# Moving half of a weight load from GpSimd's DMA queue to SyncE's, with the rounding on ScalarE

## The chip, the core and the metric

The kernel runs on one core of a Trainium2 chip. A core has five engines that run their own instruction streams in order and meet at semaphores: TensorE (PE, matrix products), VectorE (DVE), ScalarE (ACT), GpSimd (POOL) and SyncE (SP), which here only issues DMAs. Sixteen DMA engines move data between the chip's memory (HBM) and the core's on-chip memory (SBUF). The metric is the device time of one execution in microseconds; the profile also gives the span from the first to the last instruction.

## What is computed

The input is q, k and v with batch 8, 8 heads, 576 positions and head size 64, all float32. Two attentions are added: one on means over groups of 4 positions, repeated 4 times, and one at full length in a band of 3 positions to each side. The sum, as 4608 tokens of 512 numbers, goes through two products with a SiLU between them.

```python
q_d = q.reshape(B, H, Sd, 4, D).mean(axis=3)           # k_d, v_d the same
out_up = np.repeat(softmax(scale * q_d @ k_d.T) @ v_d, 4, axis=2)
mask = np.abs(pos[:, None] - pos[None, :]) < 4
out_local = softmax(np.where(mask, scale * q @ k.T, -1e9)) @ v
x = (out_up + out_local) as (4608, 512)
h = x @ w_in                                            # w_in (512, 2048)
out = (h / (1 + exp(-h))) @ w_out                       # w_out (2048, 512)
```

## The kernel before

The attention runs over 32 pairs of heads. For each pair p SyncE loads q and k (`lq`, `lk`, 288 KB each) and v in four overlapping windows (`lv`, `lv.1` to `lv.3`, 80 KB each, tile `vs`). GpSimd casts q and k to bf16 (`c`, line 544, tile `qkb`) and v (`cw`, line 554, tile `vb`), and adds pairs of q for the means (`mq`, lines 597 and 599). TensorE transposes (`T`), and ScalarE takes the result out of PSUM (`eq`, `ek`). TensorE makes the scores (`S`), ScalarE the exponentials (`x`, `xd`), VectorE masks them (`k`, line 628), TensorE makes the softmax sums (`Z`) and the products with v (`PV`; `VP` with `ev` makes the means of v). VectorE inverts the sums (`r`) and, for the first ten pairs, splits the inverse into three bf16 parts (`rx`, `rm`, `rl`, lines 711 to 714, with `rh` on ScalarE); TensorE broadcasts them (`RB`), ScalarE copies the broadcast out (`eb`, line 735, tile `Rb`). VectorE multiplies (`m`, line 745, tile `xo`), and GpSimd adds the two attentions into the token tile `xT` (`a`, line 769).

The feed-forward part takes blocks j of 512 tokens: 16 products `g1_j_f` (4 matmuls each, over the quarters kc of the 512 inputs) give 128 hidden rows f each. Each needs the tanh `t` on ScalarE (line 783) and the product `s` on VectorE (line 785), which fills `gT[j % 2]`. Then `g2` multiplies with w_out. Only two PSUM tiles, HP, take turns for `g1`.

The weights come as eight DMAs issued by GpSimd (`load_w`, line 520): `w0` to `w3` bring 512 columns of w_in each, 1 MB, into `w_in_sb`, whose type float32r is a float32 rounded for TensorE, and `w4` to `w7` bring w_out as bf16. `g1_j_f` waits for the chunk f // 4.

The order on every engine is made ahead of the run. `Plan` keeps units of work with an engine, an estimated cost, a priority and an earliest time (`ready`); `order` walks through simulated time, picks for each engine the best of its next units, and then each engine's stream is emitted in that order. A list in `FIRST` for an engine fixes its first units by name; in this kernel `FIRST` is empty. The name of a unit that comes several times gets a suffix, so `lv5.3` is the fourth `lv5`. The order that results around 20 to 50 us, for what follows:

- SyncE: per pair `lq lk lv lv.1 lv.2 lv.3`, pairs in turn
- GpSimd: `... c4 w0 cw3 mq3 c5 a0 cw4 mq4 w1 c6 a1 cw5 mq5 a2 w2 c7 cw6 mq6 a3 c8 cw7 w3 a4 ...`
- ScalarE: `... eq5 ek5 eb2 rh3 ev3 x4 xd4 eq6 ek6 eb3 rh4 ev4 x5 xd5 eq7 ek7 eb4 rh5 ev5 t0_0 t0_1 x6 ...`
- TensorE: `... S4 T6 PV3 RB3 Z4 VP4 S5 T7 Z5 RB4 VP5 PV4 g1_0_0 g1_0_1 S6 ...`
- VectorE: `... r3 mk5 m2 rx3 rm3 rl3 k4 r4 mk6 rx4 m3 rm4 k5 rl4 r5 mk7 rx5 m4 rm5 rl5 s0_0 s0_1 ...`

Of the kernel before, what the change touches and what calls it, by code (L numbers as in the profile page):

```python
# [276 lines left out]
def bass_hourglass_attn__then__act_silu_kernel(  # L277
# [9 lines left out]
    with kctx:  # L287
# [16 lines left out]
        xT = sb("xT", [128, 4, XR], F32)
        gT = sb("gT", [128, 16, 512], BF16, 2)
# [45 lines left out]
        rH = [R("h0", True), R("h1", True)]  # L351

        def one(eng, name, cost, fn, r=(), w=(), dma=None, prio=None, dcost=0.0):
            u = L.unit(eng, name, cost, prio, dcost)
            L.op(u, fn, r, w, dma)
            return u

        def mm(u, out_, lhsT, rhs, r, w, start=True, stop=True):
            L.op(u, lambda t: t.matmul(out_, lhsT, rhs, start=start, stop=stop, skip_group_check=True), r, w)  # L359
# [103 lines left out]
        def dma(eng, name, out_, in_, w, sem, dcost, r=(), prio=None, cost=0.42):  # L463
            return one(eng, name, cost, lambda s: s.dma_start(out_, in_), r, w, sem, prio, dcost)  # L464
# [42 lines left out]
        def load_vq(p):  # L507
# [67 lines left out]
        def after_T(p):  # L575
# [163 lines left out]
        def xblk(kc, t0, t1):  # L739
            return [R(f"x{kc}_{t % (XR // 64)}") for t in range(t0 // 64, t1 // 64)]  # L740
# [33 lines left out]
        def g1(j, f):  # L774
            n = ng1[0]
            ng1[0] += 1
            hb, tb = n % 2, n % 2
            t0 = (512 * j) % XR
            u = L.unit("PE", f"g1_{j}_{f}", 0.934)
            for kc in range(4):  # L780
                mm(u, hps[hb], w_in_sb[:, kc, 128 * f:128 * f + 128], xT[:, kc, t0:t0 + 512].bitcast(F32R),
                   [R(f"w_in{f // 4}")] + xblk(kc, 512 * j, 512 * j + 512), [rH[hb]], start=(kc == 0), stop=(kc == 3))
            one("ACT", f"t{j}_{f}", 0.62, lambda e: e.activation(th[tb][:, :], hps[hb], AF.Tanh, scale=0.5),  # L783
                r=[rH[hb]], w=[R(f"th{tb}")], prio=-1)
# [71 lines left out]
        def feed():  # L856

            for p in range(NPAIR):
                for name, fn, need in (
                    ("lqk", load_qk, ("c", NQK)), ("c", cast, ("T", NB - 1)),  # L860
                    ("lv", load_v, ("cw", NVS)), ("cw", castw, ("PV", NV)),
                    ("lvq", load_vq, ("cv", NVQ)), ("cv", castv, ("PV", NV)),
                ):
                    src = {"c": "lqk", "cw": "lv", "cv": "lvq"}.get(name)
                    if p < NVP and name in ("lvq", "cv"):
                        made.add((name, p))
                    if (name, p) in made or (src and (src, p) not in made):
# [105 lines left out]
```

The softmax here doesn't subtract the row's maximum and nothing guards it: scores larger than these inputs give would overflow.

## Time and profile before

| | before |
|---|---|
| device time, median of 3 (lowest, highest) | 358.56 us (356.95, 358.87) |
| span of the profiled execution | 356.2 us |
| busy: PE, DVE, ACT, POOL | 327.2, 228.1, 181.8, 156.8 us |
| chain that ended last: PE, DVE, DMA, SyncE's queue, ACT | 79, 7, 4, 4, 3% |
| w_in chunks: issues, size, median to landing | 4, 1024 KB, 10.6 us |
| the same, w_out chunks | 4, 512 KB, 11.2 us |
| vs loads: issues, size, median to landing | 126, 80 KB, 4.2 us |
| moved by DMA | 60.28 MB |

In the profile's lines L12 means line 12 of the kernel, "out<-in" names the tiles, and "[3.55 <-X]" says that the engine stood idle for 3.55 us before this instruction, until X released it. A timeline row has start, length, engine, line, operation, tiles, shapes and count. DMA issues on SyncE are told as "SPq"; "landing" is the time from the start of the issue to the completion.

### The profile page before, as it was taken

What the parts mean: (1) busy time and instruction counts of PE and PEld (TensorE: products, weight loads), DVE (VectorE), ACT (ScalarE), POOL (GpSimd) and SP (SyncE); (2) the same over time, 40 slices, a digit from 0 to 9 for tenths busy, and PEclk for the clock granted to TensorE, in tenths of its full rate; (3) what the DMA queues carried; (4) which work ended last, traced back from release to release, by engine and by line L of the source; (5) the groups of instructions that cost most, each with busy time, mean ns of one, the idle gap of its engine ahead of it and who ended that gap; (6) DMA issues with size and microseconds to landing.
All of it is one profiled execution on the core that took longest, in us unless ns stands there. A gap on an engine that the chain in (4) does not pass through costs nothing.

```text
span 356.2 us, 11025 instructions
## 1 busy us (share of the span) xinstructions
PE 327.2 (92%) x4742; PEld 212.7 (60%) x4742; DVE 228.1 (64%) x392; ACT 181.8 (51%) x326; POOL 156.8 (44%) x203
## 2 busy tenths in 40 slices
PE   1574599899999999999999999999999999999996
PEld 0453477666666666666666665666665666666642
DVE  7589889876667777777776766677754434343400
ACT  2766478766554555555555554555543343434321
POOL 7977874272374675664667367555111100000000
PEclk9998689999999999999999999999999999999999
DMA  8999999946878877778887987873222000110012
GB/s 230 248 264 243 302 297 219 220 131 179 235 193 237 223 225 223 221 201 226 233 227 193 229 240 206 194 182 107 65 111 77 31 29 29 51 39 29 31 59 88
DMA packets 73506, 60.28 MB, mean 169 GB/s; under 512 B 47986, under 2 KB 55794, under 8 KB 73458
## 3 DMA queue, kind: packets, MB, share of 16 engines
q1 hardware_dynamic: 63818, 44.27, 47.5%
q10 hardware_dynamic: 5416, 9.02, 8.7%
q0 software_dynamic: 4224, 6.29, 7.5%
q8 instruction: 37, 0.61, 0.7%
q14 instruction: 11, 0.09, 0.1%
HBM read 51.76 MB, written 9.91 MB: 173 GB/s over the span
## 4 chain that ended last, share of the span: by engine, by line
PE 79%; DVE 7%; DMA 4%; SPq 4%; ACT 3%; issue 2%; POOL 1%; POOLq 0%; ACTq 0%; DVEq 0%
PE HP L359 35%; PE o L359 25%; PE pe_ L359 8%; PE CD L359 5%; SPq L464 4%; PE AB L359 3%; DMA vq<-in_v_dram 3%; PE o L572 1%; DVE rrest L711 1%; DVE rp L714 1%; DMA vs<-in_v_dram 1%; DVE Pt L628 1%; DVE xo L745 1%; DVE zr L707 1%; DVE gT L785 1%
## 5 line engine op out<-in xcount | busy, mean ns | idle before, releaser
L785 DVE SCALAR_TENSOR_TENSOR gT<-th,HP 128x512 bf16<-128x512 f32 x144 | 96.6, 684 | 101.2 <-ACT th L783 100.8
L359 PE MATMUL HP<-xT,w_in_sb 128*128 128x512 f32 x576 | 160.0, 416 | 1.6 <-DVE gT L785 0.7
L783 ACT ACTIVATE th<-HP 128x512 f32<-128x512 f32 x144 | 86.2, 599 | 75.3 <-PE HP L359 73.4
L359 PEld LDWEIGHTS HP<-xT,w_in_sb 128*128 128x128 f32 x576 | 106.0, 189 | 28.9 <-DVE gT L785 1.3
L359 PE MATMUL o<-w_out_bf,gT 128*128 128x512 bf16 x464 | 107.0, 380 | 0.0
L359 PEld LDWEIGHTS o<-w_out_bf,gT 128*128 128x128 bf16 x464 | 42.6, 98 | 54.3 <-issue 8.6
L769 POOL TENSOR_TENSOR xT<-xo 128x576 fp32r<-128x576 f32 (+3 forms) x48 | 42.9, 907 | 44.5 <-DVE xo L745 44.5
L800 ACT ACTIVATE osb<-o 128x512 f32<-128x512 f32 x29 | 17.4, 599 | 60.4 <-PE o L359 60.3
L559 POOL TENSOR_TENSOR vt<-vq 128x512 f32<-128x512 f32 x18 | 23.0, 1278 | 56.0 <-DMA vq<-in_v_dram 55.9
L544 POOL CAST qkb<-qk 128x1152 bf16<-128x1152 f32 x30 | 36.8, 1226 | 6.9 <-PE pe_ L572 4.7
L745 DVE TENSOR_TENSOR xo<-CD,Rb 128x720 f32<-128x720 f32 x30 | 27.0, 899 | 1.0 <-ACT Rb L735 0.6
L554 POOL CAST vb<-vs 128x640 bf16<-128x640 f32 x30 | 22.1, 736 | 11.3 <-PE CD L359 5.6
L572 PE MATMUL o<-idn,qkb 64*64 64x64 bf16 x576 | 17.4, 202 | 9.9 <-DVE qkb L539 6.3
L359 PE MATMUL pe_<-w_out_bf,gT 128*128 128x512 bf16 x112 | 26.4, 380 | 0.0
L586 DVE TENSOR_REDUCE kd<-kT 128x144 bf16<-128x576 bf16 x32 | 23.3, 731 | 0.9 <-ACT kT L582 0.8
L582 ACT ACTIVATE kT<-pe_ 128x576 bf16<-128x576 bf16 x32 | 21.0, 655 | 1.9
L628 DVE TENSOR_TENSOR Pt<-Pt,mask_bf 128x576 bf16<-128x576 bf16 x32 | 20.7, 647 | 0.8 <-ACT Pt L624 0.8
L624 ACT ACTIVATE Pt<-AB 128x576 bf16<-128x576 f32 x32 | 20.7, 646 | 0.6 <-PE AB L359 0.4
L572 PEld LDWEIGHTS o<-idn,qkb 64*64 64x64 bf16 x576 | 13.9, 117 | 9.7 <-DVE qkb L539 6.3
L572 PE MATMUL pe_<-idn,qkb 64*64 64x64 bf16 x576 | 16.3, 202 | 2.0 <-DVE qkb L541 1.0
L359 PEld LDWEIGHTS pe_<-w_out_bf,gT 128*128 128x128 bf16 x112 | 10.0, 98 | 13.6 <-issue 3.2
L590 DVE TENSOR_REDUCE qd<-qT 128x144 bf16<-128x576 bf16 x24 | 17.8, 742 | 0.0
(79 smaller groups left out, 311.9 us busy)
## 6 DMA issues: line engine op xcount, KB each, us to landing
vs<-in_v_dram SPq DMA_DIRECT2D x126, 80.0 KB, 4.2
qk<-in_q_dram SPq DMA_DIRECT2D x32, 288.0 KB, 3.6
out_dram<-osb SPq DMA_DIRECT2D x36, 256.0 KB, 3.3
qk<-in_k_dram SPq DMA_DIRECT2D x30, 288.0 KB, 4.8
Rb<-scr ACTq DMA_DIRECT2D x44, 180.0 KB, 4.2
vq<-in_v_dram SPq DMA_DIRECT2D x18, 256.0 KB, 5.2
w_in_sb<-in_moe_w_in_dram POOLq DMA_DIRECT2D x4, 1024.0 KB, 10.6
w_out_bf<-in_moe_w_out_dram POOLq DMA_DIRECT2D x4, 512.0 KB, 11.2
```

What stands on the lines that cost most here:

```text
L359: L.op(u, lambda t: t.matmul(out_, lhsT, rhs, start=start, stop=stop, skip_group_check=True), r, w)
L544: one("POOL", f"c{p}", 1.15, lambda g: g.tensor_copy(qkb[j][:, :, :], qk[i][:, :, :]), r=[R(f"qk{i}0"), R(f"qk{i}1")], w=[R(f"qkb{j}0"), R ...
L554: one("POOL", f"cw{p}", 0.72, lambda g: g.tensor_copy(vb[m][:, :, :], vs[i][:, :, :]), r=rr, w=[R(f"vb{m}")])
L559: one("POOL", f"va{p}", 1.3, lambda g: g.tensor_tensor(vt[:, :, :], vq[i][:, :, 0:128], vq[i][:, :, 128:256], ALU.add), r=rr, w=[R("vt")])
L572: L.op(u, lambda e, o=o, w=w, j=j: e.transpose(o, w, idn[half(j), :]), [R("id"), R(f"qkb{n}{x}")], [rE if x else rF])
L582: one("ACT", f"ek{p}", 0.68, lambda e: e.activation(kT[j][:, 3:579].rearrange("p (g r) -> p g r", r=9), pe_[:, 0:288].bitcast(BF16).rearra ...
L586: one("DVE", f"mk{p}", 0.74, lambda e: e.tensor_reduce(kd[j][:, 0:SD], kT[j][:, 3:579].rearrange("p (g r) -> p g r", r=4), AX.X, ALU.add), ...
L628: one("DVE", f"k{p}", 0.46, lambda e: e.tensor_tensor(Pt[m][:, :, :], Pt[m][:, :, :], mask_bf[:, :].unsqueeze(1).to_broadcast([128, 2, 288 ...
L745: one("DVE", f"m{p}", 0.92, prio=-450000 if L.boost else None, r=rCD + [R(f"Rb{u}0"), R(f"Rb{u}1")], w=[R(f"xo{x}")], fn=lambda e: e.tenso ...
L769: one("POOL", f"a{p}", 0.15 + n * 0.0019, lambda g, dst=dst, in0=in0, in1=in1: g.tensor_tensor(dst, in0, in1, ALU.add), r=[R(f"xo{x}")], w ...
L783: one("ACT", f"t{j}_{f}", 0.62, lambda e: e.activation(th[tb][:, :], hps[hb], AF.Tanh, scale=0.5), r=[rH[hb]], w=[R(f"th{tb}")], prio=-1)
L785: one("DVE", f"s{j}_{f}", 0.71, lambda e: e.scalar_tensor_tensor(gT[j % 2][:, f, :], th[tb][:, :], 1.0, hps[hb], ALU.add, ALU.mult), r=[rH ...
```

## The change

The first two of the four chunks of w_in no longer come through GpSimd. Each comes as four plain float32 loads of 128 rows by 512 columns (256 KB) on SyncE's queue (`wi0`, `wi0.1` to `wi1.3`), placed among the loads of pairs 5 to 7. They land in the storage of `gT[0]`, which holds nothing until the first `s`, and ScalarE copies each with a rounding to float32r into its place in `w_in_sb` (`wr0` to `wr1.3`). `g1` now waits for each quarter kc by itself. GpSimd issues `w2` to `w7` only. The purpose is to take work from GpSimd and large transfers from among the attention's loads. `FIRST` is filled with a list per engine that covers the head of the kernel.

```diff
+NWH = 2
+WK = 1
+WSTEP = 2.0
+WT0 = 20.0
+WPRIO = 2000
 FIRST = {
+    "PE": """
...
+        VP4 S5 T7 Z5 RB4 g1_0_0 VP5 PV4 g1_0_1 S6 T8 g1_0_2 g1_0_3 RB5 Z6 g1_0_4 S7 g1_0_5 PV5 VP6 g1_0_6
...
+    "ACT": """
...
+        eb1 rh2 ev2 x3 xd3 eq5 ek5 wr0 eb2 rh3 wr0.1 ev3 wr0.2 x4 xd4 wr0.3 eq6 ek6 wr1 eb3 rh4 wr1.1 ev4
+        wr1.2 x5 xd5 wr1.3 eq7 ek7 eb4 rh5 ev5 t0_0 t0_1 x6 xd6 eq8 t0_2 t0_3 eb5 ek8 rh6 t0_4 x7 xd7 t0_5
...
+    "POOL": """
...
+        cw2 c4 cw3 mq3 c5 a0 cw4 mq4 c6 a1 cw5 mq5 a2 w2 c7 cw6 mq6 a3 c8 cw7 w3 a4 mq7 c9 cw8 w4 c10 w5 a5
...
+    "SP": """
...
+        lq4 lk4 lv3 lv3.1 lv3.2 lv3.3 lq5 lk5 lv4 lv4.1 lv4.2 lv4.3 lq6 lk6 wi0 lv5 lv5.1 wi0.1 lv5.2 lv5.3
+        wi0.2 lq7 lk7 wi0.3 lv6 lv6.1 wi1 lv6.2 lv6.3 wi1.1 lq8 lk8 wi1.2 lv7 lv7.1 wi1.3 lv7.2 lv7.3 lq9
...
 }
...
+        def load_w_in(c, a, ready):
+            i = 8 * c + 2 * a
+            d = w_in_sb[:, a:a + WK, 512 * c:512 * c + 512]
+            st = gT[0][:, i:i + 2 * WK, :].rearrange("p a b -> p (a b)").bitcast(F32).rearrange("p (a b) -> p a b", b=512)
+            sr = [R(f"g0_{f}") for f in range(i, i + 2 * WK)]
+            src = moe_w_in[128 * a:128 * a + 128 * WK, 512 * c:512 * c + 512].rearrange("(kc p) f -> p kc f", p=128)
+            dma("SP", f"wi{c}", st, src, sr, f"wi{c}_{a}", 0.82 * WK, prio=-1000).ready = ready
+            one("ACT", f"wr{c}", 0.12 + 0.43 * WK, lambda e: e.activation(d, st, AF.Copy), r=sr, w=[R(f"w_in{c}_{a}")],
+                prio=WPRIO)
...
         def load_w(c):
             if c < 4:
...
-                           [R(f"w_in{c}")], f"w_in{c}", 3.1, cost=0.9)
+                           [R(f"w_in{c}_{a}") for a in range(0, 4, WK)], f"w_in{c}", 3.1, cost=0.9)
...
-                   [R(f"w_in{f // 4}")] + xblk(kc, 512 * j, 512 * j + 512), [rH[hb]], start=(kc == 0), stop=(kc == 3))
+                   [R(f"w_in{f // 4}_{kc // WK * WK}")] + xblk(kc, 512 * j, 512 * j + 512), [rH[hb]], start=(kc == 0), stop=(kc == 3))
...
-        for c in range(8):
+        for i in range(4 * NWH // WK):
+            load_w_in(i * WK // 4, i * WK % 4, WT0 + WSTEP * i * WK)
+        for c in range(NWH, 8):
             load_w(c).ready = float((18, 25, 32, 39, 50, 56, 62, 68)[c])
```

More of the change, by code (lines that the diff above doesn't have):

```diff
@@ L164 @@
 FIRST = {
+    "PE": """
+        T0 T1 S0 T2 S1 Z0 VP0 T3 Z1 RB0 PV0 VP1 S2 T4 PV1 RB1 Z2 VP2 S3 T5 PV2 Z3 RB2 VP3 S4 T6 PV3 RB3 Z4
+        VP4 S5 T7 Z5 RB4 g1_0_0 VP5 PV4 g1_0_1 S6 T8 g1_0_2 g1_0_3 RB5 Z6 g1_0_4 S7 g1_0_5 PV5 VP6 g1_0_6
+        RB6 T9 Z7 g1_0_7 g1_0_8 S8 PV6 VP7 g1_0_9 g1_0_10 RB7 T10 Z8 g1_0_11 g1_0_12 S9 PV7 VP8 g1_0_13
+        g1_0_14 RB8 g1_0_15 g1_1_0 g1_1_1 V10 g1_1_2 g1_1_3 VP9 g2_0_0_0 g2_0_0_1 g2_0_0_2 RB9 g2_0_0_3
+        g1_1_4 g1_1_5 V11 g1_1_6 g1_1_7 VP10 g2_0_1_0 g2_0_1_1""",
@@ new lines @@
+    "ACT": """
+        lkx lk0 ckx eq0 ek0 cw0 eq1 ek1 cw1 x0 xd0 eq2 ek2 x1 xd1 ev0 rh0 eq3 ek3 eb0 rh1 ev1 x2 xd2 eq4 ek4
+        eb1 rh2 ev2 x3 xd3 eq5 ek5 wr0 eb2 rh3 wr0.1 ev3 wr0.2 x4 xd4 wr0.3 eq6 ek6 wr1 eb3 rh4 wr1.1 ev4
+        wr1.2 x5 xd5 wr1.3 eq7 ek7 eb4 rh5 ev5 t0_0 t0_1 x6 xd6 eq8 t0_2 t0_3 eb5 ek8 rh6 t0_4 x7 xd7 t0_5
+        ev6 t0_6 eb6 eq9 ek9 rh7 t0_7 t0_8 x8 xd8 ev7 t0_9 t0_10 eb7 eq10 ek10 rh8 t0_11 t0_12 x9 xd9 ev8
+        t0_13 t0_14 eb8 t0_15 t1_0 t1_1 eq11 ek11 rh9 t1_2 t1_3 x10 xd10 ev9 eb9 o0_0 t1_4 t1_5 ek12 x11 z10
+        t1_6 t1_7 xd11""",
@@ new lines @@
+    "DVE": """
+        const const.1 const.2 const.3 const.4 const.5 const.6 const.7 const.8 const.9 const.11 const.10
+        const.12 const.14 const.13 const.15 const.16 const.17 const.18 const.19 const.20 const.21 const.22
+        const.23 zero const.24 const.25 const.37 const.38 const.39 const.40 const.41 const.67 const.70
+        const.68 const.71 cq0 const.26 const.27 cq1 ck0 ck1 const.62 const.63 const.64 const.65 mk0 mk1 k0
+        mk2 r0 k1 rx0 rm0 rl0 r1 mk3 m0 rx1 rm1 rl1 k2 r2 mk4 rx2 m1 rm2 k3 rl2 r3 mk5 m2 rx3 rm3 rl3 k4 r4
+        mk6 rx4 m3 rm4 k5 rl4 r5 mk7 rx5 m4 rm5 rl5 s0_0 s0_1 k6 mq8 s0_2 r6 s0_3 mk8 rx6 s0_4 rm6 k7 rl6 m5
+        s0_5 s0_6 r7 mq9 mk9 rx7 s0_7 rm7 s0_8 rl7 k8 m6 s0_9 s0_10 r8 mq10 mk10 rx8 s0_11 rm8 s0_12 rl8 k9
+        m7 s0_13 s0_14 s0_15 s1_0 s1_1 r9 m8 mk11 rx9 s1_2 rm9 s1_3 rl9 mq11 k10 s1_4 s1_5 r10 eq12 mk12
+        mq12 s1_6""",
@@ new lines @@
+    "POOL": """
+        const.28 const.31 const.29 const.32 const.30 const.33 const.34 const.35 const.36 const.66 const.69
+        const.42 const.43 const.44 const.45 const.46 const.47 const.48 const.49 const.50 const.51 const.52
+        const.53 const.54 const.55 const.56 const.57 const.58 const.59 const.60 const.61 mq0 c2 mq1 c3 mq2
+        cw2 c4 cw3 mq3 c5 a0 cw4 mq4 c6 a1 cw5 mq5 a2 w2 c7 cw6 mq6 a3 c8 cw7 w3 a4 mq7 c9 cw8 w4 c10 w5 a5
+        w6 cw9 w7 a6 a7 c11 cw10 c12 cw11 cw12 c13 a8 a8.1 a8.2 c14 cw13""",
@@ new lines @@
+    "SP": """
+        lq0 lq1 lk1 lv0.1 lv0.2 lv0.3 lq2 lv0e lv0 lk2 lv1 lv1.1 lv1.2 lv1.3 lq3 lk3 lv2 lv2.1 lv2.2 lv2.3
+        lq4 lk4 lv3 lv3.1 lv3.2 lv3.3 lq5 lk5 lv4 lv4.1 lv4.2 lv4.3 lq6 lk6 wi0 lv5 lv5.1 wi0.1 lv5.2 lv5.3
+        wi0.2 lq7 lk7 wi0.3 lv6 lv6.1 wi1 lv6.2 lv6.3 wi1.1 lq8 lk8 wi1.2 lv7 lv7.1 wi1.3 lv7.2 lv7.3 lq9
+        lk9 lv8 lv8.1 lv8.2 lv8.3 lq10 lk10 lv9 lv9.1 lv9.2 lv9.3 lq11 lk11 lv10 lv10.1 lv10.2 lv10.3 lv11
+        lv11.1 lv11.2 lv11.3 lq12 lk12 lq13 lk13 lv12 lv12.1 lv12.2 lv12.3 lq14 lk14 lv13 lv13.1 lv13.2
+        lv13.3 out0_0 lq15 lk15 lv14 lv14.1 lv14.2""",
```

## The prediction

> **What bounds the kernel now.** I read the page first, its strip of 40 slices (8.9 us each):
>
> ```profile
> PE   1574599899999999999999999999999999999996
> ...
> PEclk9998689999999999999999999999999999999999
> DMA  8999999946878877778887987873222000110012
> ```
>
> TensorE is full from the ninth slice on, the DMA engines only up to there. The table by stretches sharpens it (after span and length: busy time of PE, PEld, DVE, ACT and POOL, then the granted clock, DMA share, GB/s):
>
> ```profile
> 20.00:30.00 10.00, 7.38 (x288) 6.07 (x285) 8.45 (x16) 7.41 (x16) 5.97 (x9) 1.00 1.13 270
> 30.00:40.00 10.00, 5.06 (x187) 4.09 (x187) 8.78 (x10) 4.91 (x12) 9.18 (x12) 0.66 1.24 276
> 40.00:50.00 10.00, 7.09 (x136) 5.69 (x137) 8.79 (x13) 4.95 (x11) 7.90 (x10) 0.83 1.23 284
> ...
> 76.00:200.00 124.00, 124.00 (x1981) 81.31 (x1981) 90.70 (x145) 68.02 (x122) 70.19 (x80) 1.00 0.76 209
> ```
>
> From 76 us on TensorE has no hole for 124 us, and only 0.67 us of them in 200 to 300. So a microsecond won or lost before about 50 us reaches the end at full value, and nothing later matters. In 30 to 50 us TensorE lacks 4.94 + 2.91 = 7.9 us, at clocks of 0.66 and 0.83. I followed the timelines of the engines there. GpSimd:
>
> ```profile
> 23.60 1.20 POOL L769 TENSOR_TENSOR xT<-xo 128x576 fp32r<-128x576 f32 x1
> 28.35 0.77 POOL L554 CAST vb<-vs 128x640 bf16<-128x640 f32 x1 [3.55 <-DMA vs<-in_v_dram]
> ...
> 30.19 0.78 POOL L464 DMA_DIRECT2D w_in_sb<-in_moe_w_in_dram  x1
> 30.97 1.16 POOL L544 CAST qkb<-qk 128x1152 bf16<-128x1152 f32 x1
> ...
> 33.91 0.65 POOL L597 TENSOR_TENSOR vt<-qT 128x288 f32<-128x288 bf16 x1
> 34.64 0.42 POOL L599 TENSOR_TENSOR qd<-vt 128x144 bf16<-128x144 f32 x1
> ```
>
> GpSimd stands 3.55 us for the values of pair 4, then runs without a gap. VectorE beside it:
>
> ```profile
> 31.00 3.66 DVE L711 SCALAR_TENSOR_TENSOR rrest<-rp,sgn,zr 128x72 f32<-128x72 bf16 x1
> ...
> 35.16 1.16 DVE L714 SCALAR_TENSOR_TENSOR rp<-rp,sgn,rrest 128x72 bf16<-128x72 bf16 x1
> ```
>
> The same two operations take 0.28 us elsewhere (26.77 and 28.26 us). The chain of waits passes through both ("31.08 3.59", then 1.17 us); they hold the broadcast RB3, which starts at 36.37. ScalarE sits idle behind it:
>
> ```profile
> 37.19 0.77 ACT L735 ACTIVATE Rb<-AB 128x720 f32<-128x720 f32 x1 [3.29 <-PE AB L359]
> ...
> 44.10 0.77 ACT L735 ACTIVATE Rb<-AB 128x720 f32<-128x720 f32 x1 [2.72 <-PE AB L359]
> ...
> 47.32 0.60 ACT L783 ACTIVATE th<-HP 128x512 f32<-128x512 f32 x1 [2.02 <-PE HP L359]
> ```
>
> These are eb3, eb4 and t0_0; the first product s0_0 follows at 47.95. Last, the landing of vs loads issued in 13 to 18 us and in 18 to 22 us:
>
> ```profile
> DMA to landing us min/median/max: 2.6/3.4/3.8
> ...
> DMA to landing us min/median/max: 7.1/7.4/7.7
> ```
>
> Between them GpSimd issued w0 (19.40 us, landed 7.9 us later): a megabyte in front of pair 4.
>
> **What the skill says.** "DMA: Bandwidth & Descriptors", section "SWDGE vs HWDGE vs iDMA": a float32r destination always casts, and only GpSimd's DMAs cast; hence the detour over a plain load and ScalarE. Same page, "Queues, rings and completion order": the write that completes a DMA lands after every earlier write of that DMA engine, across queues. The trace agrees: lv4.1, issued while w0 was, landed at 27.10, and w0 at 27.27. "SBUF — State Buffer", "Who interferes with whom": a VectorE instruction with two SBUF inputs blocks against a GpSimd instruction that reads SBUF; PE and ACT wait for nobody. The trace agrees: rrest reads rp and zr from SBUF, and its 3.66 us end in GpSimd's one small gap (34.56 to 34.64). "ScalarE: Activation LUTs", "What ACT_TABLE_LOAD costs": an ACTIVATE takes 186 + 0.833 N ns and overlaps the next by 93, so 613 ns for N = 512, 520 in a row. The trace has 599 for a 128x512 copy out of PSUM; none from SBUF.
>
> **The change, part by part.** *GpSimd loses w0 and w1*: 0.91 + 0.78 us of issuing. More comes from the landing. Pair 4's last load goes out at 21.06 to 21.74; with 3.4 to 4.1 us, as before w0, it lands at about 25.2 and cw4 runs then, not at 28.35: 3.1 us. With w1's 0.78, c6 can start near 27.2, not 30.97 (its k load, issued 22.85, lands near 26.8 without w0): 3.8 us. T6, which waits 1.6 us for c6, no longer does. GpSimd has a hole again where it waits for pair 5 (landing near 30), so rx3 should be blocked for at most one or two casts, some 0.3 to 1.3 us in place of 3.66. Together RB3 could start near 33.2 instead of 36.37: 3.2 us gained there.
>
> *SyncE gains eight issues*. A row of the same shape, an output store of 128x512 f32, takes 0.47 us, with gaps 0.51: 8 x 0.51 = 4.1 us. Between lk6 (end 23.29) and wi1.3 stand 14 old issues, which took 11.2 us before (23.34 to 34.48), 2.3 us of it pauses. So wi1.3 goes out between 36.2 and 38.5; I take 37. The bytes are the same 2 MB; they no longer come as two lumps.
>
> *ScalarE gains eight casts*: 8 x 0.52 = 4.2 us, in a stretch (28 to 48 us) where it idles 0.44 + 1.00 + 3.29 + 0.43 + 0.22 + 2.72 + 2.02 = 10.1 us, so the work itself would hide. The waits need not. ScalarE is in order: behind wr0.1 stands ev3 (for T6), behind wr1 eb3 (for S5 and m3), behind wr1.2 x5 (for k5, Z5), behind wr1.3 eq7, ek7 and then eb4, on which m4 and S6 wait. The early ones are free or cost one cast: wi0 to wi0.2 land by 31, at the time they are read. The late ones set the pace. A load lands 3.4 to 4.1 us after issue where nothing is in front, 8 to 11 us where a GpSimd megabyte is (8.0 in 31 to 36 us, 11.2 in 36 to 41). GpSimd now issues w2 some 3 us sooner, near 33, ahead of wi1.2 and wi1.3. So wi1.3 lands between 36.2 + 4 = 40.2 and 38 + 8 = 46; I take 37 + 6 = 43.
>
> *Then* wr1.3 ends at 43.6, eq7 and ek7 (0.53 each) at 44.7, eb4 at 45.5, against 44.87 before: the 3.2 us are spent, 0.6 more too. *g1_0_0 goes ahead of VP5 and PV4*: before, t0_0 waited 2.02 us while PE ran VP5, PV4 and g1 in turn. Now g1_0_0 is done by 45 and t0_0 can follow rh5 and ev5 at 46.1. s0_0 has m4 (0.91, from 45.6), rm5 and rl5 (0.29, or 1.26 if blocked) ahead on VectorE: 47.0 unblocked against 47.95, near 1 us sooner. I add 0.3 for a GpSimd with less to issue. *The pinned order* repeats the order of before save for these insertions, read off the lists; it costs nothing by itself. *Separate waits for each quarter of w_in, staging in the first g buffer*: nothing, since s0_0 writes it long after wr0 has read it.
>
> Sum: 1.3 us sooner, 358.56 - 1.3 = 357.3.
>
> **The rivals.** A: *the landings keep up*. If w2 doesn't get ahead of them (40.2 for wi1.3), eb4 starts near 42.2, and s0_0 near 44.8, 3.2 us sooner: 355.4. For it: loads that no lump delays land in 3.4 us. Against it: w2's lump moves up towards them, and DMA share is above 1.1 all through. B: *the casts' wait replaces the broadcast's*. If both last loads get w2 in front, wi1.3 at 46 puts eb4 at 47.7 and t0_0 near 49.4, 2.1 us later: 360.7. For it: 8 and 11 us in the rows of that time, and SyncE's pauses (1.83 us at 25.31) come back with longer landings. Against it: the total is no more than before. C: *DMA-paced anyway*, 358.5: GpSimd's casts wait 0.74, 0.32 and 0.18 us for pairs 6 to 8. These are too small to carry it.
>
> **How the numbers follow.** Forecast 0.45 (two thirds of it inside 1.8 us, one third beyond on the fast side), A 0.27, B 0.23, C 0.05. Faster by over 0.5%: 0.15 + 0.27 = 0.42; within: 0.30 + 0.05 = 0.35; slower: 0.23. The range goes 1.2 us below A, as clock and blocked VectorE operations add to a gain, and 0.3 above B: 354.2 to 361.0.
>
> **What would show it.** Right: the 3.55 us wait of vb shrinks below 1.5; no rrest of over 2 us near 31; ScalarE waits for a DMA ahead of a w_in_sb copy for 2 us or more in 35 to 45 us; eb4 stays within a microsecond or so of 44.1. Wrong to the fast side: no such wait, s0_0 before 45.5. Wrong to the slow side: wi1.3 lands after 45, or rrest is blocked as long at another place. A hole of TensorE after 76 us would break the one-for-one step.

## The result, and the profile after

The changed kernel takes 362.21 us (median of 4, 361.53 to 364.70) where the kernel before takes 357.75 in the same runs: a ratio of 1.0148, 95% interval 1.0107 to 1.0189. It is slower by 4.5 us by the medians. The prediction, 357.3 with a range up to 361.0, was wrong. The ratios leave out executions in a slower state and are not quotients of the medians (here 1.0125). The later series ran on different chips, each with the kernel before beside it; across series it is the ratios that can be compared. One profile is one execution, and the executions of one kernel spread over some 2 us to each side of their median (the kernel before: 355.4 to 361.0 in a later series), so a difference of a microsecond or two between two traces proves nothing by itself.

The strip of the page after, 40 slices of 9.0 us:

```profile
PE   0586379999999999999999999999999999999996
...
PEclk9999999999999999999999999999999999999999
DMA  8987999944687877878897788873122000010012
```

TensorE is full from the seventh slice on here. Its dip is in slices four and five, and in this execution the granted clock is at full speed in every slice, so a throttled clock isn't the reason for its time. In the kernel before, too, the clock makes no such difference: of its 212 executions in the later series, the 35 with a mean granted clock of 0.995 or more have a median of 358.2 us, the 152 with less than 0.978 one of 358.0. The table by stretches (columns as before: PE, PEld, DVE, ACT, POOL, clock, DMA share, GB/s):

```profile
20.00:30.00 10.00, 8.37 (x260) 6.98 (x260) 8.24 (x14) 7.13 (x16) 7.82 (x11) 1.00 0.83 234
30.00:40.00 10.00, 6.33 (x158) 5.20 (x162) 8.31 (x11) 6.72 (x14) 6.32 (x9) 1.00 0.85 241
40.00:50.00 10.00, 4.50 (x94) 3.43 (x95) 3.96 (x9) 5.08 (x11) 4.85 (x7) 1.00 1.16 308
50.00:76.00 26.00, 24.93 (x502) 18.83 (x501) 23.39 (x43) 19.91 (x40) 12.50 (x14) 1.00 1.15 246
76.00:200.00 124.00, 122.63 (x1965) 80.74 (x1978) 90.64 (x143) 67.29 (x121) 72.44 (x83) 1.00 0.76 206
```

In 40 to 50 us TensorE is busy for 4.50 us where it was for 7.09 (at a clock of 0.83), and VectorE for 3.96 where it was for 8.79. Most of the lost time lies there: `eb3` ahead of this stretch is 1.4 us late (38.62 against 37.19), `s0_0` behind it 5.85. From 20 to 40 us the DMA engines are less busy than before (0.83 and 0.85 against 1.13 and 1.24). From 76 us on TensorE is all but full, as before (122.63 of 124 us, with 1965 matmul records against 1981).

GpSimd's rows. The start of `cw4`, `c6`, `cw6`, `c8` and `cw7` in turn:

```profile
26.53 0.71 POOL L605 CAST vb<-vs 128x640 bf16<-128x640 f32 x1
...
28.32 1.14 POOL L595 CAST qkb<-qk 128x1152 bf16<-128x1152 f32 x1
...
39.29 0.72 POOL L605 CAST vb<-vs 128x640 bf16<-128x640 f32 x1 [1.64 <-DMA vs<-in_v_dram]
...
43.90 1.14 POOL L595 CAST qkb<-qk 128x1152 bf16<-128x1152 f32 x1 [1.08 <-DMA qk<-in_k_dram]
47.64 0.72 POOL L605 CAST vb<-vs 128x640 bf16<-128x640 f32 x1 [2.60 <-DMA vs<-in_v_dram]
```

The 3.55 us wait ahead of `cw4` is gone and `c6` starts at 28.32, 2.65 us sooner than before (30.97). But the later casts now wait for the loads of pairs 6 to 8. VectorE, pair 3's split of the inverse and then `k5` and `rl4`:

```profile
34.27 0.28 DVE L762 SCALAR_TENSOR_TENSOR rrest<-rp,sgn,zr 128x72 f32<-128x72 bf16 x1
34.58 1.12 DVE L764 CAST rp<-rrest 128x72 bf16<-128x72 f32 x1
35.74 2.01 DVE L765 SCALAR_TENSOR_TENSOR rp<-rp,sgn,rrest 128x72 bf16<-128x72 bf16 x1
...
46.32 0.46 DVE L679 TENSOR_TENSOR Pt<-Pt,mask_bf 128x576 bf16<-128x576 bf16 x1 [4.68 <-ACT Pt L675]
46.70 0.29 DVE L765 SCALAR_TENSOR_TENSOR rp<-rp,sgn,rrest 128x72 bf16<-128x72 bf16 x1
```

`rx3` takes 0.28 us in place of 3.66. The operations after it are blocked instead, and then VectorE stands 4.68 us for `x5`. ScalarE shows why (`eb3`, `wr1.2`, `x5`, `wr1.3`, `eb4`, `t0_0`; then `x5` of the kernel before):

```profile
38.62 0.77 ACT L786 ACTIVATE Rb<-AB 128x720 f32<-128x720 f32 x1 [0.31 <-PE AB L400]
...
45.12 0.63 ACT L568 ACTIVATE w_in_sb<-gT 128x512 fp32r<-128x512 f32 x1 [4.14 <-DMA gT<-in_moe_w_in_dram]
45.66 0.63 ACT L675 ACTIVATE Pt<-AB 128x576 bf16<-128x576 f32 x1
...
46.84 0.63 ACT L568 ACTIVATE w_in_sb<-gT 128x512 fp32r<-128x512 f32 x1
...
48.44 0.77 ACT L786 ACTIVATE Rb<-AB 128x720 f32<-128x720 f32 x1
...
51.13 0.59 ACT L834 ACTIVATE th<-HP 128x512 f32<-128x512 f32 x1
```

```profile
39.22 0.65 ACT L624 ACTIVATE Pt<-AB 128x576 bf16<-128x576 f32 x1 [0.22 <-PE AB L359]
```

The first SiLU product `s0_0` follows, 5.85 us later than before (its row holds `s0_1` too):

```profile
53.80 1.27 DVE L836 SCALAR_TENSOR_TENSOR gT<-th,HP 128x512 bf16<-128x512 f32 x2
```

The chain of waits of the kernel after goes through the same place (start, length, what):

```profile
38.15 6.95 DMA gT<-in_moe_w_in_dram
...
45.12 0.63 ACT w_in_sb L568
45.75 0.55 ACT Pt L675
...
46.32 0.47 DVE Pt L679
...
46.84 0.63 PE CD L400 x14
47.47 0.71 PE AB L400 x10
48.18 1.86 PE HP L400 x4
50.04 0.77 PE pe_ L400 x7
50.81 0.74 PE CD L400 x23
51.58 0.91 DVE xo L796
```

The load `wi1.2` goes out at 38.15 and lands at 45.10; then come the cast `wr1.2`, `x5`, the mask `k5`, pair 5's softmax sums, RB4, `g1_0_0`, VP5, PV4 and `m4`. SyncE's queue shows how late the loads went out. First the kernel after (`wi1.2`, two `vs`, `wi1.3`, two `vs`, `lq9`), then the kernel before, where the same `lq9` starts 6.5 us sooner:

```profile
38.15 0.68 SPq L505 DMA_DIRECT2D gT<-in_moe_w_in_dram  x1
38.88 1.38 SPq L505 DMA_DIRECT2D vs<-in_v_dram  x2
40.30 0.72 SPq L505 DMA_DIRECT2D gT<-in_moe_w_in_dram  x1
41.06 1.27 SPq L505 DMA_DIRECT2D vs<-in_v_dram  x2
42.38 0.61 SPq L505 DMA_DIRECT2D qk<-in_q_dram  x1
```

```profile
35.85 0.96 SPq L464 DMA_DIRECT2D qk<-in_q_dram  x1
```

A second series of the changed kernel, and another trace of it:

> The changed kernel once more, beside the others on this chip: ratio to before 1.011 to 1.019 as measured first, with ScalarE waiting for wi1.2 or wi1.3 ahead of x5 or eq7 in the trace again.

It took 364.10 us, ratio 1.0174 (1.0125 to 1.0222). In the trace above two casts wait, 4.5 us together; in this one all eight do. The waits of ScalarE in it (total us, times, longest):

```profile
ACT w_in_sb L568 <- DMA gT<-in_moe_w_in_dram: 11.9, 8, 4.7
```

So how much the early casts wait differs from one execution to the next; the wait ahead of `x5` (4.14 and 4.7 us) is there in both. The granted clock differs too. In this trace it is half of full speed in the stretch where the trace above has 1.00:

```profile
30.00:40.00 10.00, 4.22 (x123) 3.39 (x123) 4.26 (x7) 5.95 (x12) 5.72 (x8) 0.52 1.03 289
40.00:50.00 10.00, 2.79 (x89) 2.44 (x90) 2.70 (x6) 3.93 (x10) 4.47 (x6) 0.50 1.06 257
```

### The profile page after: what moved, and what is told of

Its sections match the earlier page's. It is cut to its first block, busy times and chain, and to the rows that moved or that the text cites. A ratio compares the mean times of both kernels' runs of the same rounds, so it can differ in the third digit from the quotient of the medians.

```text
span 359.6 us, 11008 instructions
## 1 busy us (share of the span) xinstructions
PE 329.0 (91%) x4712; PEld 215.9 (60%) x4742; DVE 226.2 (63%) x392; ACT 185.8 (52%) x334; POOL 155.0 (43%) x201
## 4 chain that ended last, share of the span: by engine, by line
PE 82%; DVE 5%; SPq 4%; DMA 4%; ACT 2%; issue 1%; POOL 0%; ACTq 0%; POOLq 0%
PE HP L400 37%; PE o L400 28%; PE pe_ L400 8%; PE CD L400 5%; SPq L505 4%; PE AB L400 3%; DMA vs<-in_v_dram 2%; DMA gT<-in_moe_w_in_dram 2%; PE o L623 1%; DVE gT L836 1%; DVE rp L765 1%; DVE Pt L679 1%; ACT Pt L675 0%; DVE xo L796 0%; DVE qd L641 0%
## 5 line engine op out<-in xcount | busy, mean ns | idle before, releaser
L400 PE MATMUL o<-w_out_bf,gT 128*128 128x512 bf16 x437 | 101.5, 379 | 1.7
L595 POOL CAST qkb<-qk 128x1152 bf16<-128x1152 f32 x30 | 35.7, 1190 | 10.1 <-PE pe_ L623 5.8
L679 DVE TENSOR_TENSOR Pt<-Pt,mask_bf 128x576 bf16<-128x576 bf16 x32 | 21.8, 682 | 6.5 <-ACT Pt L675 6.5
```

Of the source, the lines that this page charges most:

```text
L595: one("POOL", f"c{p}", 1.15, lambda g: g.tensor_copy(qkb[j][:, :, :], qk[i][:, :, :]), r=[R(f"qk{i}0"), R(f"qk{i}1")], w=[R(f"qkb{j}0"), R ...
L679: one("DVE", f"k{p}", 0.46, lambda e: e.tensor_tensor(Pt[m][:, :, :], Pt[m][:, :, :], mask_bf[:, :].unsqueeze(1).to_broadcast([128, 2, 288 ...
```

## The experiments

**The theory.** The in-order ScalarE waits for loads that SyncE sends too late, and what is queued behind the casts holds up TensorE (rival B's mechanism). Against it: the order put on the engines; the work of the casts; the loads themselves, through SyncE's queue and the DMA engines; and w2 in front of the late loads.

### The order alone, and the work without the loads

`e2_order` is the kernel before with the lists of the change, less the `wi` and `wr` units, and with w0 and w1 in their old places on GpSimd.

```diff
 FIRST = {
+    "PE": """
...
+        VP4 S5 T7 Z5 RB4 g1_0_0 VP5 PV4 g1_0_1 S6 T8 g1_0_2 g1_0_3 RB5 Z6 g1_0_4 S7 g1_0_5 PV5 VP6 g1_0_6
```

> The kernel before, with the changed kernel's pinned order (w0 and w1 put back at their old places on GpSimd, g1_0_0 ahead of VP5 and PV4 on TensorE) and nothing else of the change. Theory W: the order by itself costs nothing, 357.8 us within 0.8. Rival O (g1_0_0 ahead of VP5 and PV4 delays PV4, m4 and through them the next products): 1.5 to 3 us slower than before, 359.5 to 361.

Measured: 358.14 us, ratio 1.0020 (0.9997 to 1.0044). The order by itself explains at most a small part.

`e7_noload` is the changed kernel without its eight loads; the casts read a constant, so half of w_in is neither loaded nor used.

```diff
-            dma("SP", f"wi{c}", st, src, sr, f"wi{c}_{a}", 0.82 * WK, prio=-1000).ready = ready
+            st = idn[:, :].unsqueeze(1).to_broadcast([128, 8, 64])
+            sr = [R("id")]
```

> The changed kernel without the eight wi loads; the eight roundings stay at their places on ScalarE but read a constant, so half of w_in is not loaded. It leaves ScalarE's eight operations and takes away their waits, SyncE's issues and 2 MB of transfers. Theories W and S: at or below the time before, 355 to 357.5, x5 near 39 us. Rival A (ScalarE's 4.2 us of work itself delays eb2, ev3, x4, eb3): stays at 360 or above.

Measured: 355.06 us, ratio 0.9921 (0.9889 to 0.9952). With the casts in place and GpSimd relieved, but no loads, the kernel is faster. So neither the 4.2 us of ScalarE's work nor the lists are what costs.

`e12_unread` puts the loads back, into storage of their own that nothing reads, and keeps the constant (half of w_in is loaded and not used): SyncE and the DMA engines have the whole traffic, and no cast waits for it.

```diff
-            st = gT[0][:, i:i + 2 * WK, :].rearrange("p a b -> p (a b)").bitcast(F32).rearrange("p (a b) -> p a b", b=512)
+            st = stg[:, (4 * c + a) % 5, 0:512]
```

> The changed kernel with all eight wi loads issued and moved as they are, but landing in storage that nobody reads; the eight roundings stay at their places and read a constant, so half of w_in is loaded and not used. Nothing waits for the wi loads any more; SyncE's issues and the 2 MB stay. Theory W (the waits of ScalarE for the landings carry the loss): 356.5 to 358, ratio 0.996 to 1.001, x5 before 41 us. Rival S (what SyncE's extra issues do to the attention's own loads carries it): above 360, GpSimd's waits for pairs 5 to 7 as long as in the changed kernel.

Measured: 357.73 us, ratio 1.0013 (0.9986 to 1.0040). The three kernels split the change: relief of GpSimd, with lists and casts, 0.9921; the loads being there adds 0.9% (1.0013 less 0.9921), and the relief is used up; the casts' waiting for them adds another 1.35 to 1.6% (1.0148 and 1.0174 less 1.0013). Each of these shares is good to some 0.5%, by the intervals. The last is as large as the whole slowdown.

### The place of the casts

`e1_late` moves only `wr1.2` and `wr1.3` behind `ev5` and `t0_0`; `e9b_late` moves all eight, to where their loads have landed or nearly so. The loads stay. The edit of `e9b_late`:

```diff
-        eb1 rh2 ev2 x3 xd3 eq5 ek5 wr0 eb2 rh3 wr0.1 ev3 wr0.2 x4 xd4 wr0.3 eq6 ek6 wr1 eb3 rh4 wr1.1 ev4
-        wr1.2 x5 xd5 wr1.3 eq7 ek7 eb4 rh5 ev5 t0_0 t0_1 x6 xd6 eq8 t0_2 t0_3 eb5 ek8 rh6 t0_4 x7 xd7 t0_5
+        eb1 rh2 ev2 x3 xd3 eq5 ek5 eb2 rh3 ev3 x4 xd4 wr0 eq6 ek6 wr0.1 eb3 rh4 ev4 wr0.2
+        x5 xd5 wr0.3 eq7 ek7 eb4 rh5 ev5 wr1 t0_0 wr1.1 t0_1 wr1.2 x6 xd6 eq8 wr1.3 t0_2 t0_3 eb5 ek8 rh6 t0_4 x7 xd7 t0_5
```

> The changed kernel, with the last two roundings moved behind ev5 and t0_0 in ScalarE's order, so that x5, eq7, ek7 and eb4 no longer stand behind them. Theory W (ScalarE's in-order wait for wi1.2, 4.14 us, makes the loss): x5 starts near 41.3 us instead of 45.66, the first gT product near 49.5 instead of 53.80, and the time falls by about 4 us, to 358. Rival S (SyncE's eight more issues delay the attention's own loads, and GpSimd's waits for them carry the loss): GpSimd's waits stay, the first gT product stays after 52.5, the time above 360.5.

> The changed kernel with nothing but the roundings moved late in ScalarE's order (wr0 to wr0.3 behind xd4, ek6, ev4 and xd5, wr1 to wr1.3 behind ev5, t0_0, t0_1 and eq8); eight loads, GpSimd's order as it is. Theory W: the waits for landings are nearly gone, ratio 0.996 to 1.003. If the eight issues on SyncE cost something of their own through GpSimd's wait for pair 6 ahead of a3, it stays 1 us or more above the run with two loads and a3 ahead, which was 0.998.

Measured: 359.37 us, ratio 1.0037 (1.0011 to 1.0063), with two casts moved; 357.79 us, ratio 0.9995 (0.9973 to 1.0017), with all. ScalarE's rows in `e9b_late` (`x5`, `t0_0`, `wr1.2`):

```profile
36.84 0.69 ACT L675 ACTIVATE Pt<-AB 128x576 bf16<-128x576 f32 x1
...
43.75 0.59 ACT L834 ACTIVATE th<-HP 128x512 f32<-128x512 f32 x1
...
46.92 0.63 ACT L568 ACTIVATE w_in_sb<-gT 128x512 fp32r<-128x512 f32 x1 [1.57 <-DMA gT<-in_moe_w_in_dram]
```

`wi1.2` lands as late as in the changed kernel (46.9), but `x5` has been done for nine microseconds. So the slowdown comes from where the casts stand in ScalarE's queue: the late load is there in both kernels, and only what is queued behind its cast is held up.

`e15_dose` asks whether one wait of this size at this place is enough. It is `e2_order` with one more ScalarE copy ahead of `x5`, whose result nothing uses, reading the window of v that the load `lv7.3` brings.

```diff
-        x5 xd5 eq7 ek7 eb4 rh5 ev5 t0_0 t0_1 x6 xd6 eq8 t0_2 t0_3 eb5 ek8 rh6 t0_4 x7 xd7 t0_5
+        ws x5 xd5 eq7 ek7 eb4 rh5 ev5 t0_0 t0_1 x6 xd6 eq8 t0_2 t0_3 eb5 ek8 rh6 t0_4 x7 xd7 t0_5
```

> The kernel before in the pinned order (w0 and w1 on GpSimd as before, no wi, no roundings), with one added ScalarE copy of 64x320 right ahead of x5 that reads the fourth window of v of pair 7, which lands near 46.2 us; the copy's result is not used. It gives the kernel before only the one wait. Theory W: x5 moves from 39.7 to near 46.7 us, the first gT product comes 5 to 6 us later, and the kernel is 4 to 5.5 us slower than before, ratio 1.011 to 1.016, as the changed kernel. Rival S or any account by GpSimd's relief, SyncE's issues or bytes: within 1 us of the pinned order alone.

ScalarE's rows of it:

```profile
44.19 0.47 ACT L914 ACTIVATE osb<-vs 64x320 f32<-64x320 f32 x1 [4.06 <-DMA vs<-in_v_dram]
44.68 0.65 ACT L660 ACTIVATE Pt<-AB 128x576 bf16<-128x576 f32 x1
```

Measured: 360.68 us, ratio 1.0095 (1.0063 to 1.0127), just under the expected band, with a landing 2 us earlier than expected. A wait of 4.06 us ahead of `x5`, with nothing else of the change but the order, costs 0.75% (1.0095 less 1.0020), about half of the slowdown. `e1_late` puts the two late casts higher, at 1.1% (1.0148 less 1.0037), and leaves 0.4% for the six earlier ones (1.0037 less the 0.9995 of `e9b_late`; 5 waits, 6.1 us in its trace). The dose was somewhat smaller: `x5` starts at 44.68 with it, at 45.66 and 47.42 in the two traces of the changed kernel.

### Why the loads are late

`e4_w2late` issues w2 behind `mq6` and `a3`, after the last `wi`. `e8_two` makes each chunk one load of 1 MB on SyncE, at the places of `wi0` and `wi1`, with six issues fewer.

```diff
-        cw2 c4 cw3 mq3 c5 a0 cw4 mq4 c6 a1 cw5 mq5 a2 w2 c7 cw6 mq6 a3 c8 cw7 w3 a4 mq7 c9 cw8 w4 c10 w5 a5
+        cw2 c4 cw3 mq3 c5 a0 cw4 mq4 c6 a1 cw5 mq5 a2 c7 cw6 mq6 a3 w2 c8 cw7 w3 a4 mq7 c9 cw8 w4 c10 w5 a5
```

> The changed kernel with w2 issued behind a3 on GpSimd, some 6 us later, so that no GpSimd megabyte is in front of wi1.2 and wi1.3. Theory L (w2 in front makes the late landing): wi1.2 lands 4 us after its issue instead of 6.9, ScalarE waits near 1.2 us instead of 4.14, the time falls by about 3 us, to 359. Theory P (SyncE's pace makes it: wi1.2 is issued only at 38.15): the wait stays above 3 us and the time within 1 us of 362.

```diff
-            src = moe_w_in[128 * a:128 * a + 128 * WK, 512 * c:512 * c + 512].rearrange("(kc p) f -> p kc f", p=128)
+            src = moe_w_in[:, 512 * c:512 * c + 512].rearrange("(kc p) f -> p kc f", p=128)
```

> The changed kernel with each chunk as one load of 1 MB on SyncE, at the places of wi0 and wi1, and the eight roundings where they are: six issues less, the same bytes. Theory W: wi1.2's data arrives near 39 us and not 45.1, the wait ahead of x5 falls from 4.14 to under 1 us, while wr0 may wait up to 2 us for its whole megabyte: 358 to 359.5. If SyncE's issue slots are not what delays the landing: 361 or more.

Measured: 360.97 us, ratio 1.0075 (1.0050 to 1.0100), for w2 late; `wi1.2` still landed 7.1 us after its issue (36.65 to 43.7). The megabyte in front isn't what makes the landing slow. Neither expectation came out whole: the issue came 1.5 us sooner, the wait ahead of `x5` fell to 2.17 us (8.0 us for all casts), and half of the slowdown is gone. `e8_two`: 360.89 us, ratio 1.0103 (1.0068 to 1.0137), above the 358 to 359.5 of theory W. There `wr1.2` ahead of `x5` waits for nothing, but the first cast of each chunk waits, 3.11 us for the megabyte that lands at 31.9 and 1.51 for the second, and `eb2` behind the first starts at 32.50 (before the change: 29.30). The wait has moved to other casts.

`e13_tiny` is `e12_unread` with 16 columns to a load (8 KB in place of 256 KB); again the loads are read by nobody.

> As the run with unread loads, but each wi load brings 16 columns (8 KB) and not 512 (256 KB), so the eight issues of SyncE stay and the 2 MB of transfers go. If the issue slots of SyncE are what the attention's loads lose: within 1 us of the run with unread loads. If it is the bytes in the DMA engines: near the run without loads, 355, and clearly below the run with unread loads.

Measured: 359.36 us, ratio 1.0045 (1.0014 to 1.0075): no better than the full loads (1.0013, and the two intervals overlap), and nowhere near 355. So taking 2 MB of transfers away gives nothing back, and the bytes are not what uses up the relief. That the issues do is what is left, and isn't shown by itself. Two things can be read from the trace. First SyncE's queue, the row of `lq9`, in `e7_noload` (no `wi` issues) and in `e13_tiny`:

```profile
36.47 1.68 SPq L505 DMA_DIRECT2D qk<-in_q_dram  x1
```

```profile
40.24 0.61 SPq L506 DMA_DIRECT2D qk<-in_q_dram  x1
```

Between the end of `lk6` and the start of `lq9` lie 11.7 us without `wi` issues (before: 12.6), 17.0 with eight small ones, 17.7 in `e12_unread` and 18.8 in the changed kernel. Over more traces it is 11.7 to 12.6 us in the four without `wi` issues and 16.3 to 18.8 in the eight with all eight full loads, so eight issues cost SyncE's stream some 4 to 7 us, and a share of their bytes doesn't show. Second, the landings of the small loads (us from issue, minimum, median, maximum):

```profile
DMA to landing us min/median/max: 2.0/3.3/7.7
```

An 8 KB load issued at 35.85 lands 7.3 us later. Why the kernel isn't faster than `e12_unread` is not settled. In its trace VectorE's operations with two SBUF inputs (`rx`, `rl`, `k`) are blocked for longer (9.4 us over their shortest times in 18 to 56 us, against 5.6), but the kernel before, no slower than either, has 11.1.

### The order on TensorE

The trace of the changed kernel shows 1.86 us of `g1_0_0` ahead of PV4 in the chain, and `m4` waiting 1.89 us for PV4. Three runs put VP5 and PV4 first again: in the changed kernel, in `e9b_late`, and in `e9_best` (next section).

```diff
-        VP4 S5 T7 Z5 RB4 g1_0_0 VP5 PV4 g1_0_1 S6 T8 g1_0_2 g1_0_3 RB5 Z6 g1_0_4 S7 g1_0_5 PV5 VP6 g1_0_6
+        VP4 S5 T7 Z5 RB4 VP5 PV4 g1_0_0 g1_0_1 S6 T8 g1_0_2 g1_0_3 RB5 Z6 g1_0_4 S7 g1_0_5 PV5 VP6 g1_0_6
```

> The changed kernel with one thing undone: on TensorE VP5 and PV4 stand ahead of g1_0_0 again, as before the change. Theory 'the order was not free': in the changed kernel m4 stood 1.89 us for PV4, behind the 1.86 us of g1_0_0, and s0_0 stood behind m4; with the old order m4 starts when eb4 is done (near 49.3 instead of 51.58), s0_0 is then set by t0_0 and starts near 52.2 instead of 53.8, and the time falls by 0.7 to 1.6 us, to a ratio of 1.011 to 1.013. Rival 'TensorE has the same work either way': s0_0 moves, s0_15 stays near 77.3 and the ratio stays at 1.015 to 1.017. The wait of 4 us ahead of x5 stays in both.

> The changed kernel with its eight casts moved late (as in e9b_late, ratio 0.9995) and VP5 and PV4 ahead of g1_0_0 on TensorE. Theory 'the order was not free': 0.3 to 0.7 us below e9b_late, 0.9975 to 0.999. Rival: within 0.1 per cent of it.

> The version with two 1 MB loads, late casts and a3 ahead of cw6 (e9_best, ratio 0.9979) with VP5 and PV4 ahead of g1_0_0 on TensorE. Theory 'the order was not free': 0.996 to 0.9975, which with five rounds would be below the kernel before by more than its interval. Rival: 0.998 again.

Measured: 363.51 us, 1.0153 (1.0120 to 1.0186); 358.06 us, 1.0003 (0.9975 to 1.0031); 357.05 us, 0.9982 (0.9961 to 1.0003). Each agrees with its partner in the other order (1.0148 and 1.0174; 0.9995; 0.9979). So this part of the change is neutral, within intervals of some 0.3%. The traces can't say more: `s0_0` of `e20_late_pe` starts 3.7 us later than that of `e9b_late` (48.38 against 44.71), but these two executions also differ in time (359.49 and 357.37), as the two series don't.

### Looking for a version that is faster than both

`e9_best` takes two 1 MB loads, late casts, and `a3` ahead of `cw6`. `e14_best2` moves the two loads behind the windows of pairs 5 and 6; `e16_best3` moves the second behind `lk8`; `e18_best4` also issues w2 behind `c8`. The core of the last, as against the changed kernel:

```diff
-        wi0.2 lq7 lk7 wi0.3 lv6 lv6.1 wi1 lv6.2 lv6.3 wi1.1 lq8 lk8 wi1.2 lv7 lv7.1 wi1.3 lv7.2 lv7.3 lq9
+        wi0 lq7 lk7 lv6 lv6.1 lv6.2 lv6.3 lq8 lk8 wi1 lv7 lv7.1 lv7.2 lv7.3 lq9
...
-        cw2 c4 cw3 mq3 c5 a0 cw4 mq4 c6 a1 cw5 mq5 a2 w2 c7 cw6 mq6 a3 c8 cw7 w3 a4 mq7 c9 cw8 w4 c10 w5 a5
+        cw2 c4 cw3 mq3 c5 a0 cw4 mq4 c6 a1 cw5 mq5 a2 c7 a3 cw6 mq6 c8 w2 cw7 w3 a4 mq7 c9 cw8 w4 c10 w5 a5
```

> The run with two loads, with every rounding moved late in ScalarE's order (wr0 to wr0.3 behind xd4, ek6, ev4 and xd5, wr1 to wr1.3 behind ev5, t0_0, t0_1 and eq8) and a3 ahead of cw6 on GpSimd. If the waits ahead of ev3, eb3 and x5 and GpSimd's wait for pair 6 ahead of a3 were the whole loss, the gain of a GpSimd without w0 and w1 comes through: 355 to 357, faster than before. If not: 358 or above.

> The run with two loads and late roundings, with the two loads placed later on SyncE (behind lv5.3 and lv6.3, so that pair 5's values land ahead of the first megabyte) and wr0 to wr0.3 behind ek6, rh4, ev4 and xd5. GpSimd's wait of 3.3 us for pair 5 should fall below 1 us. If that wait held what is left of the gain, 354.5 to 356 us, ratio below 0.995. If it is hidden, as with two loads before: 0.998.

> The run with two late-placed loads, with wi1 behind lk8 on SyncE instead of ahead of lq8. If the loads of pair 8 take the gain back: c8's wait of 5.1 us falls by 2 to 3 us, the sixteenth gT product of the first block comes 1 to 2 us sooner than 71.2, 355.5 to 356.5 us, ratio 0.994 to 0.997. If something else does: within 0.2% of 0.999.

> The same with w2 issued behind c8 on GpSimd, so that neither megabyte is in front of pair 8's q and k. If the loads of pair 8 take the gain back: c8 starts near 39.5 us with a wait under 1 us, and the time is 354.5 to 356, ratio 0.990 to 0.996, near the run without loads (0.992), unless the later w2 makes g1_0_8 wait. If something else does: 0.998 or above with c8 early all the same.

Measured: 356.72 us, 0.9979 (0.9947 to 1.0011); 357.49, 0.9993 (0.9959 to 1.0028); 357.12, 0.9992 (0.9965 to 1.0020); 357.14, 0.9976 (0.9942 to 1.0010). All are well below the changed kernel; none can be told from the kernel before, and the last two fall short of what their expectations have for loads taking the gain back. One reading is that the relief doesn't arrive because the attention's own loads, queued behind the `wi` loads on SyncE, come later. GpSimd's casts `c8` and `cw7` in `e9b_late`, and `cw7` in `e16_best3`:

```profile
46.17 1.14 POOL L595 CAST qkb<-qk 128x1152 bf16<-128x1152 f32 x1 [4.22 <-DMA qk<-in_k_dram]
49.56 0.72 POOL L605 CAST vb<-vs 128x640 bf16<-128x640 f32 x1 [2.25 <-DMA vs<-in_v_dram]
```

```profile
46.83 0.72 POOL L604 CAST vb<-vs 128x640 bf16<-128x640 f32 x1 [4.08 <-DMA vs<-in_v_dram]
```

Before, these two casts waited 0 and 0.32 us. Moving the second load behind `lk8` takes the wait from `c8` and gives it to `cw7`. `s0_0` starts at 43.29 in `e14_best2`, 4.7 us sooner than before, but the sixteenth product `s0_15` at 71.19, only 1.6 sooner, and the medians differ by 0.4 us (the traced execution, 355.43, is the fastest of its series). That pairs 7 and 8 arriving later takes the gain back is what these waits point to; `e16_best3` and `e18_best4` only moved the wait, and no run removed it with the loads in place, so it isn't shown. By its own expectation `e16_best3` speaks for something other than pair 8's loads: `c8` no longer waits, and the ratio is still within 0.2% of 0.999.

## Why the prediction was wrong

**The step that failed** is the landing of the late loads: "I take 37 + 6 = 43" for `wi1.3`. Measured: issued at 40.30, landed 6.5 us later, at 46.82. The landing time was right; the issue was 3.3 us too late. It wasn't the chance of one execution: in all eight traces with the full loads `wi1.3` goes out at 39.2 to 41.2, later than the stated 36.2 to 38.5. The mis-sized term is "8 x 0.51 = 4.1 us" for SyncE, with the pauses of before taken as mostly gone. In the trace of the result the stretch from `lk6` to `lq9` grew by 6.3 us (12.6 to 18.8). The price of an issue was that of an output store; here seven of the eight issues took 0.61 to 0.73 us and one 2.47 (`wi0.3`, at 29.84), 7.05 us together. In other traces most `wi` issues took 0.43 to 0.61 us, near the assumed price, with single long ones among them (up to 1.65); why these are long stays open. On the time, the casts' waits cost 1.35 to 1.6% (`e12_unread`), where the forecast let the relief pay for them.

**What stood behind the cast was followed on one engine only.** The prediction names `x5` behind `wr1.2`, but takes the end of `eb4` from `wr1.3`, `eq7` and `ek7`. In the chain `x5` releases `k5`, and on VectorE `rl4`, which RB4 and so `eb4` need, stands behind `k5` ("k5 rl4" in VectorE's order). `rl4` starts at 46.70 and RB4 ends at 48.18; `ek7` on ScalarE is done as `eb4` starts, at 48.44. So `x5` alone, kept to 45.66, would have held `eb4` nearly as long. `eb4` ends at 49.21 against the forecast 45.5.

**"The early ones are free or cost one cast"** held in the trace of the result (0.32 us ahead of `wr0.3`) and not in the second one, where all eight wait, 11.9 us in all. `wi0.2`, to land by 31, landed at 33.5 even in the first. This term, put at next to nothing, is about the 0.4% between `e1_late` and `e9b_late`.

**GpSimd's relief was right in its first steps** (`cw4` 1.8 us sooner where 3.1 was forecast, `c6` 2.65 where 3.8 was, `rx3` unblocked), and of the "3.2 us gained" at RB3 nothing was there: `eb3` starts at 38.62 against 37.19. In this trace GpSimd runs `cw4` to `a1` from 26.53 to 30.63 with no gap over 0.1 us, as it had run from 30.19 to 36 before, and VectorE's blocked time moved to pair 2: `rm2`, `k3` and `rl2` took 0.81, 1.51 and 0.83 us in place of 0.19, 0.45 and 0.28, so that `eb2` came 3.3 us later and `rx3` with it. Of this, 0.6 us is in the trace already before the blocks (the inverse of pair 2 starts at 26.24 against 25.64). The Trainium skill's "SBUF — State Buffer", section "Who interferes with whom", has a VectorE instruction with two SBUF inputs blocked by a GpSimd instruction that reads SBUF; the rows of `k3` and `rl2` agree in where the blocks fall, and suggest that taking a GpSimd wait away gives VectorE fewer gaps (`rm2`, a cast with one input, is longer too, and this sentence doesn't cover it). In the second trace pair 2 is hardly blocked (`k3` 0.97, `rl2` 0.69) and `eb2` comes at 29.72, but the early casts' waits put `eb3` at 39.42 all the same. What the forecast had right is the landing: `vs` loads issued in 18 to 22 us took 4.3 us in the median, and 3.4 in `e7_noload`, in place of 7.4 (7.4 in `e2_order` too, which keeps w0). That the relief is worth something without loads in the way is shown by `e7_noload` (0.9921).

**"The bytes are the same 2 MB; they no longer come as two lumps"** was half right. Loads of v issued in 27 to 37 us landed after 4.1 us in the median where it had been 7.4. But they were issued later, and so landed later in the end: `lv7`, the first window of pair 7, at 45.5 against 41.4, `lq9` at 48.2 against 44.9. No cost was put on what stands behind the eight issues on SyncE. The runs with late casts show the bill: ratios of 0.9976 to 1.0003 where the relief alone had 0.9921.

**"A microsecond won or lost before about 50 us reaches the end at full value"** fails when it is applied to `s0_0`. TensorE still had holes in 50 to 76 us in the kernel before (24.12 us of work in 26):

```profile
50.00:76.00 26.00, 24.12 (x511) 17.89 (x509) 21.50 (x41) 19.95 (x40) 12.50 (x15) 1.00 1.16 237
```

There the advances of `s0_0` were lost: 4.7 us in `e14_best2`, 1.6 left at `s0_15`. For the slowdown `s0_0` is 5.85 us later, `s0_15` 4.5, the span 3.4 in these two traces, the medians 4.5. What does reach the end is time won or lost at `s0_15`: in all 19 traces the span ends 282.3 to 284.9 us after `s0_15` starts, but 305.8 to 310.6 after `s0_0`.

**The order** was put down as nothing by itself, which is right (1.0020, and 1.0153 against 1.0148 with it undone in part); "g1_0_0 goes ahead" as a gain didn't come: `m4`, and behind it `s0_0`, then waits for PV4, and undoing it changed nothing. **The casts' work** as hidden is right (`e7_noload`).

**The rivals.** B had the mechanism, the casts' wait in the broadcast's place, and was too small, 2.1 us later where 4.5 was measured, with 46 for `wi1.3` (measured 46.82) and `eb4` at 47.7 (measured to end at 49.21); it too left out the path over `k5`. Its reason, w2 in front of both loads, isn't needed (`e4_w2late`: 7.1 us without it). Of the signs named beforehand, "wi1.3 lands after 45" and "rrest is blocked as long at another place" marked the slow side; the first came true, the second did not (the longest blocked are `rl3`, 2.01, and `k3`, 1.51). Three signs of the right side came true as well: the wait of `vb`, `rx3` near 31, and a ScalarE wait of over 2 us; the fourth, `eb4` near 44.1, did not (48.44).

## What to carry to other kernels

A unit that waits for a DMA belongs where the data has surely landed, in the queue of an in-order engine; put ahead of other work it costs what stands behind it, on that engine and on the engines that follow. Before new loads go in front of others on a busy queue, count what they do to the loads behind: the change here freed one engine by 2.7 us and sent the attention's loads out 6.5 us later. And follow the first unit behind a wait through every engine's order, not only along the engine that waits.

## What was not expected of the hardware

- From about 36 us on the size of a load hardly set its landing. In `e13_tiny` 8 KB loads issued at 35.85 and 37.74 us took 7.3 and 7.7 us, and 80 KB loads in 36 to 41 us 7.2 to 8.8; in `e12_unread` 256 KB loads issued at 37.47 and 39.29 took 7.7. Earlier it did: the first six took 2.0 to 3.7 us with 8 KB, 3.9 to 6.4 with 256 KB. The Trainium skill's "DMA: Bandwidth & Descriptors", section "Queues, rings and completion order", has a DMA's completing write land after every earlier write of that DMA engine, across queues; these rows fit that, but none shows whose writes were in front.
- The time of a SyncE issue of one shape isn't fixed: 0.61 to 0.73 us in seven rows and 2.47 in one. Eight issues moved the stream behind them by 4.4 us with 8 KB each (17.0 less 12.6), and by 3.8 to 6.3 with 256 KB.
- The same program waited 4.5 us for its casts in one execution and 11.9 in another, and the times differed by 3.5 us (361.53 and 364.98); the mean granted clocks were 1.000 and 0.967.
